# Scratch of the spectra laid out so that one DMA of 128 partitions loads each uin and kin tile; residual loaded in pieces

## The chip, the cores and the metric

One core of one Trainium2 chip runs the program. The metric is device time in microseconds (us) of one execution; lower is better. The core's engines are TensorE (PE, with its weight loads PEld), VectorE (DVE), ScalarE (ACT), GpSimd (POOL, idle here but for the first 2 us) and SyncE (SP), which here does nothing but issue DMAs. Each engine works through its own list of instructions in order; an instruction that waits holds everything behind it on that engine, DMA issues included.

## The reference, cut to what matters

```python
x = A_u                                        # 1 x 2048 x 512, f32
xn = layernorm(x)
# branch A: state-space convolution, done in the reference with an FFT over 2L = 4096
K = einsum("dn,dnl,dn->dl", Cc, exp(dt*A*l), dt*Bc).real     # 512 x 2048, from 128 complex states
s = irfft(rfft(pad(xn.T)) * rfft(pad(K)))[:, :L].T + xn * Dskip
# branch B: a token-mixing block and an MLP
h  = gelu(layernorm(xn) @ w1)                  # 512 -> 512
hs = concat(shift(h, +1), shift(h, -1), shift(h, +2), shift(h, -2), by quarters of D) @ w2
x1 = xn + hs
b  = x1 + gelu(layernorm(x1) @ w3) @ w4        # 512 -> 1376 -> 512
out = x + s * silu(b)
```

## The kernel before, in words

Tokens are split as token = (t, r, s): 32 rows of partitions t for each of r = 0..3, and 16 steps s in the free dimension, so that the tile `X` (128 x 16 x 512) holds the whole activation. The program is recorded by a `Plan` and then issued in the order of a table of numbers (`ORDER`, one number per recorded operation); a letter behind a number says whether a copy or scaling runs on ACT or on DVE. That table decides what stands behind what on every engine. It was made for this program, and the change brings a new one.

The stages overlap by that table. (1) `loads`, layer norm, `h_pair` (w1 and gelu), `u_stage1`: the first step of the Fourier transform of the input by a small matrix `ks1`, copied out as `ue` and stored to the DRAM scratch `Ud`. (2) `hs_pair` (w2), weights w3 and w4 split into two f16 parts (`prep`), then the MLP: eight groups of 256 tokens (`mlp`), each with six steps of w3 (PE tile `pb`, gelu `g`, split `ghl`) and w4 (PE tile `pa`). (3) `tables(0)`, `tables(1)`: for each of the two halves of the channels (256 channels, "half 0" and "half 1"), eight chunks of 32 channels. DVE and ACT build the waves `wv`, PE sums them over the states (`pc`), the result `kev` goes through `ks1` on PE, is copied to `k1e` and stored to the scratch `K1d[half]`, called `scr_Kfa` and `scr_Kfb` in the profile. Two stores per chunk write 4096 runs of 64 bytes each. (4) `products(0)`, `products(1)`: units over the 32 frequencies g. Each unit loads constants `cst` (from `c_gp` for half 0, `c_gq` for half 1, two buffers in turn), `uin` from `Ud` and `kin` from `K1d`. PE forms the two spectra (half 0: `pd` from `kin` and `uin`; half 1: f16 parts `kx` and `uh`, into `pc`), ACT or DVE copies one spectrum to `kh`, DVE multiplies (`pr`), PE runs the first step of the inverse (`pd<-pr,cst`), the result `z1e` is stored to `Zd` (`scr_Zda`, `scr_Zdb`). Half 0 has 16 units of one block, half 1 has 8 units of two blocks. (5) `gate`: silu of the MLP's result in `X`; `inverse`: `zin` is loaded from `Zd`, PE runs the last step (`pd` or `pc` from `zin,is`), DVE multiplies it into `X`; `finish`: DVE adds the residual `xr` (loaded again from the input) and SP and ACT store to the output. MLP work (`pb`, `pa`) fills PE between the steps of stages 3 to 5.

A scratch tensor is one name to the planner: a load from `scr_Kfb` stands behind all sixteen stores to `scr_Kfb`. So half 1 can't load a `kin` before the last chunk of `tables(1)` has landed.

The lines that the prediction's steps touch are 450 to 454 (the scratch), 565 to 566 (buffers of `zin` and `xr`), 804 to 809 (stores of `k1e`), 844 to 852 (loads of `uin` and `kin`), 960 to 975 (`residual` and `finish`), 1121 to 1134 (`u_stage1`) and 1314 to 1323 (the end). Instructions are recorded in one helper, so the profile gives line 330 for nearly all of them and they are told apart by tile.

Of the kernel before, what the change touches and what calls it, by code (L numbers as in the profile page):

```python
# [54 lines left out]
def shape_constants():  # L55
# [10 lines left out]
    c["c_ks1"] = np.tile(np.stack([np.cos(a1), -np.sin(a1)], axis=2).reshape(L1, 2 * NG), (4, 1))  # L66
# [50 lines left out]
8 19 6 39 3 86 7 1086 2 4 44 0 1 21 5 89 90 87 88 91 92 93 94 95 22 20 10 96 97v 23 9 98a 107 108 102v 105 106  # L117
109 110 111 99a 100 101a 103 104a 145 24 26 25 27 18 35 11 33 112 34 32 113 114 115v 117v 123 124 125 116v 118
168 166 164 170 167 119a 120a 28 30 29 31 142 121 126 122a 169 165 16 13 171 143 127 172 14 173 128 174 46 129
175 176 47 177 144 48 130 146 147 178a 180a 181v 179v 78 148 79a 281 285 283 287 149a 131 152a 153a 204a 185v  # L120
150a 284 132 188 282 288 182v 133 286 134 289 201v 155 189 135 290 15 159 224 291 220 225 136 183 222 221 186
191 192 226 223 190 184a 292 187a 154 227 151 52 228 138a 536 229 537 43 230 293 231 49 366 232 50 294 233 51
194 234 53 193 295 235v 54 199a 236a 198a 368 200 207 297v 140v 210 243v 238v 195a 55 56 205 202 59 208 57 58
141 60 237v 206a 364 538 203a 196a 211 264a 367 239v 137 209 369 213 212 296v 61 217a 218a 197 162 17 247 12 374
240 244 219 365 370 62 241a 304a 245a 260a 214a 248 249 215v 63 246 298v 250 251 67 242 139 68 161 216 45 64 69
300v 253 70 539 257v 268 80 269 65 541 261 375 258a 265 252 270 262v 72 259 271 272 299v 263 371 266a 254a 255a
267 37 81a 274 71 273 163 66 73 278v 74 279v 308 84 321v 256 41 301 305 542 76 40 275v 372 160 276v 309 280 277
302v 380 75 306v 311 312 546 303 544 307 547 325v 77 36 314 313 156 319a 310 570 82 83a 315a 316a 318v 320 332
322 323a 317 373 549 85v 326 333 334 329 540 327v 324 378 548 328 345 346 543 157 550 347 571 551 552 554 553
335 42 339v 572 362 336v 358 330 430 376 337v 340v 338 348 350a 377 382 558 349a 351 341 432 388 545 158 361 433  # L130
555 573 381 575 574 331 383 363 386 452 352a 379 434 423 384 556 454 359 557 427 560 422 559 439 342 576 561 579
577 562 389 343 563a 424 578 390 387 344 428 564 565 566a 385 353a 391 591 438 567a 431 443 592 392 581 593 580
425 569 568 400 594 597 444 435 582 596 583 595 401 455 393 584a 440 429 394 354 612 402 436 395 456 441 403 445
437 396 453 464 613 614 397 585 598 355 615 446 586 404 616 587a 457 399 442 466 458 398 600 419 416 459 417a
426 405 478 480 406 588a 460 599 356 407 360 618 357 479 465 486 408 447a 418 409 461 448 462 617 410 602 463
483 420a 528a 590 449 475 589 421 529a 530 601 532a 533a 641 476a 619 450a 534 472 412 413 620 621 469 633 501
414 603 604 500 473a 634 487 531 535 643 505 451 635 502 644 474 491 751a 646 638 605a 645 730 497 731 494 732
622 733a 847 606 636 477 637 508 623 639 734 640 488 498a 737 738 607 744 499 514 608a 739 495a 609a 745 610
740a 741 624 625 746 647 626a 509a 752a 755a 735 736 411 742 627 648 831 747a 611 743 510 748 753 515a 649 756a
642 496 667 415 652 766 767 650 759 760 749 628 651 757 750 517 511 754 668 761 516 768 769a 773 629a 762a 774  # L140
653 669 670 655 518a 758 780 781 787 788 630a 512a 782 654 763 764 657 656 775a 673 671 513 519 658 659 688 660a
770 676 689 672 776 765 794 771 795 772 832 830 789 801a 690 661 796 783a 777 816 662 691 631 632 663a 664a 665
674 778 809 779 784 790a 802a 692 675 785 786 817 678 810 677 797a 791 693 805a 679 680 697 803 798 694 811 681a
792 806a 709 710 682 711 807 695 793 812a 804 813 823 492 715 818 683 837 799 696 698 712 666 800 814 824 684a
808 713 819a 714 699 825a 1296 1289 1297 826 716 820 1087 717 718 685a 1298 686 687 1088 1290 1291 1310a 700 701
815 821 822 827 720 1095 702a 1292a 703 704 1097 705a 846 1299a 1100 1092 1303 1304 1089 706a 708 707 1098 719
1091 1090 829 1293 467 828 1300 481 1311a 1093 721 722 723a 724 468 1312 863 848 1318 1094 1294 1295 1313 1301
725 1099 1319 1109 1101 1305 1122 1102 1314a 1306a 726a 727a 1307 484 729 1096 1315v 728 1302 1320 1332 1325
1326 1123 470 1308 1309 1321v 1316 1322 485 1106 1124 1103 1105 1104 1317 1107 833 834 493 1108 489 1128 1333
1125 1327 1328a 1323 1324 1329 1111 1110 1127 1346 1347 1339 1340 835 865 1330 1331 849 1334a 866 836a 850 838  # L150
864 482 490 1126 1348 839 471 520 840 841 1112 1113 1114a 1129 1144 842 521 522 1335 1130 862 844a 843a 845 523
1341 1145 1342a 1146 1368 851 853 1369 852a 1336 1349a 1353 1354 1115 854 855 856 857 1131 1343 879 880 1116
1147 1355 1132 858 859a 1360a 860a 881 861 882 1117 1118a 867 1119a 1121 1133 1338 868a 1350 1337 897 1361a 869
870 871 1134 1135 1166 1362 1364a 1136a 895 1137 878 872 1344 1345 1363 873 1356v 1351 1167 1120 1150 1153 1168
1149 1138 874 876a 1139 1357 875a 885 898 896 911 1148 883 913 894 884a 877 1169 1171 886 1352 888 1375 887 889
1376 1358 890 1365a 1151 506 1170 1366 1367 1152 1172 1154 1155 891a 892a 1359 1370 901 1140a 899 1377 927 914
929 1382 900a 1141a 902 893 903 1143 904 905 1383 1371a 1196 1389 910 1378a 1396 1390 912 1173 1372 906 907a
908a 1156 1188 1157 1189 909 1158a 915 1174 917 943 916a 1190 1397 1373 1374 930 1159 1160 1175 1379 918 920 926
928 1198 1199 919 1384v 921 1197 1201 1191 945 1142 922 923a 924a 925 946 1161 931 961 944 1385 1176 1177 932a
1200 1162a 933 1391 942 1380 1163a 959 960 934 936 1193 1165 935 937 1194 1192 1195 1381 1386 938 940a 939a 1398  # L160
1202 1178 1179 1392a 947 977 1203 1388 1387 1164 949 962 1204 1403 1393 978 1210 958 941 975 948a 1418 1404 950
952 951 953 1410a 1223 1207 1205 1206 1224 1405 1225 1399v 1400 507 954 955a 1419 1394 1395 1411v 963 976 956a
974 993 1412 1414a 965 1425 1401 1402 1180a 1208 957 964a 966 1181 967 969 1406a 1226 968 1182 1420 991 1407
# [268 lines left out]
def kernel(  # L432
# [41 lines left out]
    class Ring:  # L474
# [3 lines left out]
        def __call__(self, shape, dt, name):  # L478
            o = self.o + self.size * (self.k % self.bufs)
            self.k += 1  # L480
            return at(o, shape, dt, name)
# [869 lines left out]
```

## Time and profile before

| | |
|---|---|
| three runs | 550.22, 554.72, 553.86 us; median 553.86 us |
| the profiled execution | 549.37 us, span of the core 547.6 us, mean granted TensorE clock 0.994 |
| busy: PE, DVE, ACT | 520.5, 491.8, 429.2 us |
| DMA | 91.40 MB in 210781 packets, 155104 of them under 512 bytes |
| HBM | 56.96 MB read, 29.36 MB written |
| issues on SP | `uin` 48 and `kin` 48, `scr_Ud` 16, `scr_Kfa` and `scr_Kfb` 32, `xr` 8 |

The span is what lies between the first and the last instruction of the core in the profile; the time of that execution is 1.8 us longer. Busy times are unions of an engine's instructions. A timeline row reads: start, duration, engine, line, operation, output and inputs, count, and in brackets how long the engine had been idle before it and what released it. Where a row stands for several instructions, its duration runs from the start of the first to the end of the last, and the next row can begin a little before that end, since matmuls are pipelined.

### The profile page before, as it was taken

The numbers are of one execution on the slowest core, as the hardware profiler recorded it, in microseconds if no ns is written. First come the engines' busy times: TensorE is split into PE (matmuls) and PEld (weight loads), VectorE is DVE, ScalarE is ACT, GpSimd is POOL, SyncE is SP. The second block draws the span as 40 slices with busy tenths as digits, with TensorE's granted clock in tenths as the row PEclk, the third lists the DMA queues.
The fourth block names the chain that finished last, engine by engine and source line by source line (L and its number), as shares of the span: only waits on it lengthen the run. The fifth ranks groups of instructions, "written<-read, shape, count | busy, mean of one in ns | idle before, by whom it ended". The sixth has DMA issues, their size and how long they took to land.

```text
span 547.6 us, 13679 instructions
## 1 busy us (share of the span) xinstructions
PE 520.5 (95%) x5660; PEld 336.6 (61%) x5660; DVE 491.8 (90%) x757; ACT 429.2 (78%) x695; POOL 0.7 (0%) x6
## 2 busy tenths in 40 slices
PE   8999989999999999999999999989999999998983
PEld 8787764544476765666656666655566666766540
DVE  4899999999999999999999899989984999896657
ACT  4799999868999999999889889967766366464630
POOL 0000000000000000000000000000000000000000
PEclk9999999999999999999999999999999999999997
DMA  8986763265847236464376676696689988997996
GB/s 213 208 266 217 232 229 125 85 118 134 135 144 145 41 40 59 60 97 60 117 122 146 135 140 173 139 143 107 134 174 170 297 261 240 294 254 224 311 293 192
DMA packets 210781, 91.40 MB, mean 167 GB/s; under 512 B 155104, under 2 KB 196064, under 8 KB 210336
## 3 DMA queue, kind: packets, MB, share of 16 engines
q1 hardware_dynamic: 206112, 86.08, 66.4%
q10 hardware_dynamic: 4608, 4.46, 2.8%
q8 instruction: 44, 0.72, 0.6%
q14 instruction: 17, 0.14, 0.1%
HBM read 56.96 MB, written 29.36 MB: 158 GB/s over the span
## 4 chain that ended last, share of the span: by engine, by line
PE 45%; DVE 21%; DMA 13%; ACT 12%; SPq 4%; issue 3%; DVEq 0%; ACTq 0%
PE pb L330 15%; PE pa L330 14%; PE pc L330 9%; PE pd L330 7%; DVE wv L330 5%; SPq L330 4%; DVE X L330 4%; ACT mag L330 4%; DMA X<-in_A_u_dram 4%; DMA cst<-c_gq 3%; DVE tm L330 2%; ACT L330 2%; DMA out_dram<-X 2%; DVE pr L330 1%; DMA scr_Zda<-z1e 1%
## 5 line engine op out<-in xcount | busy, mean ns | idle before, releaser
L330 PE MATMUL pb<-x1T,w3h 128*128 128x256 f16 (+1 forms) x1056 | 124.0, 273 | 2.0 <-ACT g L330 1.3
L330 PE MATMUL pa<-w4h,ghl 128*128 128x512 f16 (+1 forms) x528 | 121.9, 379 | 0.0
L330 PEld LDWEIGHTS <-w3h 128*128 128x128 f16 (+1 forms) x1056 | 102.1, 100 | 29.1 <-issue 14.8
L330 PEld LDWEIGHTS <-ghl 128*128 128x128 f16 (+1 forms) x528 | 49.7, 98 | 57.8 <-issue 5.3
L330 ACT ACT_TABLE_LOAD x57 | 73.1, 1283 | 2.6 <-PEq L1339 1.7
L330 ACT ACTIVATE wv<-wv 128x2080 f32<-128x2080 int32 x32 | 62.9, 1964 | 5.5 <-DVE wv L330 5.3
L330 ACT ACTIVATE g<-pb,wsc 128x512 f32<-128x512 f32 (+1 forms) x48 | 31.1, 652 | 10.7 <-PE pb L330 9.8
L330 DVE TENSOR_TENSOR wv<-wv,eg 128x2048 f32<-128x2048 f32 x16 | 36.5, 2283 | 0.0
L330 DVE TENSOR_TENSOR wv<-mag,wv 128x2048 f32<-128x2048 f32 x16 | 36.5, 2281 | 0.0
L330 PE MATMUL pd<-pr,cst 64*128 64x256 f32 x256 | 36.3, 402 | 0.0
L330 DVE SCALAR_TENSOR_TENSOR ghl<-g,wsc,ghl 128x512 f16<-128x512 f32 (+1 forms) x48 | 33.6, 699 | 2.8 <-ACT ghl L330 2.7
L330 PE MATMUL pc<-wv 128*32 128x64 f32 x2048 | 32.6, 220 | 2.4 <-issue 2.4
L330 PEld LDWEIGHTS pc<-wv 128*32 128x32 f32 x2048 | 29.8, 109 | 7.7 <-issue 5.8
L330 ACT ACTIVATE ghl<-g,wsc 128x512 f16<-128x512 f32 (+1 forms) x37 | 25.3, 687 | 10.9 <-PE pa L330 9.9
L330 ACT ACTIVATE mag<-par 128x128 f32<-128x128 f32 x132 | 33.1, 454 | 0.0
L330 ACT COPY z1e<-pd 128x256 f32<-128x256 f32 x51 | 17.2, 376 | 20.2 <-PE pd L330 17.4
L330 ACT ACTIVATE wv<-wv,halfpi 128x2080 f32<-128x2080 f32 x16 | 32.9, 2057 | 0.1
L330 ACT ACTIVATE kh<-pc,ksc 128x256 f32<-128x256 f32 (+1 forms) x37 | 18.2, 541 | 18.6 <-PE pc L330 12.6
L330 PE MATMUL pb<-xT,w 128*128 128x256 f32 x128 | 29.9, 384 | 0.7 <-ACT xT L330 0.7
L330 PEld LDWEIGHTS pd<-pr,cst 64*128 64x128 f32 x256 | 22.2, 186 | 10.9 <-issue 7.5
L330 DVE BATCH_NORM_STATS2 stats<-X 128x6 f32<-128x512 f32 x32 | 21.2, 680 | 7.1 <-DMA X<-in_A_u_dram 7.1
L330 PEld LDWEIGHTS pb<-xT,w 128*128 128x128 f32 x128 | 23.4, 190 | 6.5 <-ACT hT L330 1.1
(167 smaller groups left out, 905.5 us busy)
## 6 DMA issues: line engine op xcount, KB each, us to landing
wst<-in_B_w_dram SPq DMA_DIRECT2D x20, 512.0 KB, 4.4
scr_Ud<-ue SPq DMA_DIRECT2D x16, 512.0 KB, 3.2
scr_Kfa<-k1e SPq DMA_DIRECT2D x16, 256.0 KB, 6.3
uin<-scr_Ud SPq DMA_DIRECT2D x32, 128.0 KB, 2.9
cst<-c_gp SPq DMA_DIRECT2D x16, 256.0 KB, 3.1
kin<-scr_Kfa SPq DMA_DIRECT2D x32, 128.0 KB, 2.7
scr_Zda<-z1e SPq DMA_DIRECT2D x16, 256.0 KB, 3.4
scr_Kfb<-k1e SPq DMA_DIRECT2D x16, 256.0 KB, 5.9
```

The costliest lines, as they stand in the source:

```text
L330: ins = [getattr(self.engines[op.eng], name)(*args, **kw).ins for name, args, kw in op.calls]
```

## The change

`Ud` becomes [half, r, s, re/im, g, 256 channels] instead of [r, s, g, re/im, 512 channels]. `K1d` becomes [i, re/im, g, 256] instead of [g and re/im, i, 256]. The constant `ks1` gives its rows in the same order (all real parts, then all imaginary ones). With that, the partition index of `uin` and `kin` is one dimension of the scratch, so one DMA of 128 partitions replaces two of 64, and two (half 0) or four (half 1) frequencies lie side by side: rows of 2 and 4 KB where they were 1 KB. For it, each `ue` is stored by two DMAs with 1 KB rows instead of one with 2 KB rows, and the 64-byte runs of a `k1e` store now lie 64 KB apart along i instead of 1 KB. The residual of a half comes in four pieces of four steps instead of two of eight; half 0 has two buffers for them and three (not four) for `zin`. All operations have a new order.

```diff
-    c["c_ks1"] = np.tile(np.stack([np.cos(a1), -np.sin(a1)], axis=2).reshape(L1, 2 * NG), (4, 1))
+    c["c_ks1"] = np.tile(np.stack([np.cos(a1), -np.sin(a1)], axis=1).reshape(L1, 2 * NG), (4, 1))
...
 ORDER = """
-8 19 6 39 3 86 7 1086 2 4 44 0 1 21 5 89 90 87 88 91 92 93 94 95 22 20 10 96 97v 23 9 98a 107 108 102v 105 106
+2 5 4 0 6 8 7 86 22 21 20 23 9 10 27 87 89 88 24 26 90 25 3 91 19 11 92 93 39 18 28 31 29 30 34 35 32 33 94 16
...
-    Ud = dram.tile([4, S, NG, 2, D], F32, name="scr_Ud")
-
     DH = D // 2
-    K1d = [dram.tile([2 * NG, L2, DH], F32, name=f"scr_Kf{h}") for h in "ab"]
+    Ud = dram.tile([2, 4, S, 2, NG, DH], F32, name="scr_Ud")
+
+    K1d = [dram.tile([L2, 2, NG, DH], F32, name=f"scr_Kf{h}") for h in "ab"]
...
-    zinr = [Ring(early, K4, 4), Ring(o, K4, 8)]
-    xrs = [early + 4 * K4, o + 13 * K4, late, late + 2 * K4]
+    zinr = [Ring(early, K4, 3), Ring(o, K4, 8)]
+    xrs = [Ring(early + 3 * K4, K4, 2), Slots(o + 13 * K4, o + 14 * K4, late, late + K4)]
...
             Q.dma_start(
-                K1d[cc // 8][:, :, ch : ch + 16],
+                K1d[cc // 8][:, :, :, ch : ch + 16].rearrange("i e g d -> (e g) i d"),
                 k1e[64 * c : 64 * c + 64].rearrange("p i n d -> p i (n d)"),
             )
...
-            for e in range(2):
-                Q.dma_start(
-                    uin[e::2],
-                    Ud[:, :, g0 : g0 + 2 * nb, e, ch].rearrange("r s g d -> (r s) g d"),
-                )
+            Q.dma_start(uin, Ud[hf][:, :, :, g0 : g0 + 2 * nb].rearrange("r s e g d -> (r s e) g d"))
             kin = ring["kin"]([P, 2 * nb, DH], F32, "kin")
-            halves_of = K1d[hf][2 * g0 : 2 * g0 + 4 * nb].rearrange("(k e) i d -> e i k d", e=2)
-            for e in range(2):
-                Q.dma_start(kin[e::2], halves_of[e])
+            Q.dma_start(kin, K1d[hf][:, :, g0 : g0 + 2 * nb].rearrange("i e g d -> (i e) g d"))
...
-    def residual(hf):
+    def residual(hf, pieces):
         ch = slice(hf * DH, hf * DH + DH)
-        for k in range(2):
+        for k in pieces:
             due(f"xr{hf}.{k}")
-            xr = at(xrs.pop(0), [P, S // 2, DH], F32, "xr")
-            by_r(xr, xv[:, :, k * S // 2 : (k + 1) * S // 2, ch], load=(Q, A))
-            resid.append(xr)
+            xr = xrs[hf]([P, 4, DH], F32, "xr")
+            by_r(xr, xv[:, :, 4 * k : 4 * k + 4, ch], load=(Q, A))
+            resid[hf, k] = xr
...
-            Q.dma_start(
-                Ud[2 * rp : 2 * rp + 2, s : s + 2].rearrange("r s g e d -> (s g e) r d"), ev_t
-            )
+            for h in range(2):
+                Q.dma_start(
+                    Ud[h, 2 * rp : 2 * rp + 2, s : s + 2].rearrange("r s e g d -> (s e g) r d"),
+                    ev_t[:, :, h * DH : (h + 1) * DH],
+                )
...
     for hf in range(2):
-        residual(hf)
+        residual(hf, (1, 2) if hf == 0 else (1, 2, 3, 0))
         for k, g in enumerate(END_ORDER):
...
+            if hf == 0 and k in (1, 3):
+                residual(hf, (3,) if k == 1 else (0,))
```

`Slots` hands out the given places one after the other, as `Ring` does for a ring of buffers.

Three places of the new order. First, SP's list where half 0 ends and half 1 begins: `scr_Kfb<-k1e` are the stores of the last chunks of `tables(1)`, `uin` and `kin` with 64 or 128 partitions are the loads of the first units of half 1. Before:

```order
L330 DMA scr_Kfb<-k1e 4096x1x16
L330 DMA scr_Zda<-z1e 128x512
L330 DMA scr_Kfb<-k1e 4096x1x16
L330 DMA cst<-c_gq 128x1024
L330 DMA_TRANSPOSE x1T<-x1h 128x8x128
L330 DMA scr_Zda<-z1e 128x512
L330 DMA uin<-scr_Ud 64x4x256 x2
L330 DMA scr_Kfb<-k1e 4096x1x16 x2
L330 DMA uin<-scr_Ud 64x4x256 x2
L330 DMA kin<-scr_Kfb 64x4x256
L330 DMA uin<-scr_Ud 64x4x256
L330 DMA kin<-scr_Kfb 64x4x256
```

And now:

```order
L330 DMA cst<-c_gq 128x1024
L330 DMA uin<-scr_Ud 128x1024 x2
L330 DMA_TRANSPOSE x1T<-x1h 128x8x128
L330 DMA scr_Zda<-z1e 128x512
L330 DMA scr_Kfb<-k1e 64x64x16 x2
L330 DMA uin<-scr_Ud 128x1024
L330 DMA kin<-scr_Kfb 128x1024 x2
L330 DMA xr<-in_A_u_dram 32x4x256
L330 DMA kin<-scr_Kfb 128x1024
```

Two whole `uin` now stand ahead of the last two stores of `k1e` where one did, and one issue instead of two brings a whole `kin` behind them.

Second, SP's list in the middle of half 1, where `cst` has two buffers in turn. Before:

```order
L330 DMA scr_Zdb<-z1e 128x1024
L330 DMA uin<-scr_Ud 64x4x256
L330 DMA cst<-c_gq 128x1024
L330 DMA uin<-scr_Ud 64x4x256
L330 DMA kin<-scr_Kfb 64x4x256
L330 DMA uin<-scr_Ud 64x4x256
L330 DMA_TRANSPOSE x1T<-x1h 128x8x128
L330 DMA uin<-scr_Ud 64x4x256 x2
L330 DMA kin<-scr_Kfb 64x4x256
L330 DMA cst<-c_gq 128x1024
```

And now:

```order
L330 DMA uin<-scr_Ud 128x1024 x2
L330 DMA kin<-scr_Kfb 128x1024
L330 DMA cst<-c_gq 128x1024
L330 DMA uin<-scr_Ud 128x1024
L330 DMA scr_Zdb<-z1e 128x1024
L330 DMA xr<-in_A_u_dram 32x4x256
L330 DMA kin<-scr_Kfb 128x1024
L330 DMA cst<-c_gq 128x1024
```

Between two loads of constants stood six halves of `uin` and `kin`; now there are one `uin` and one `kin`, and a piece of the residual among them.

Third, the end of DVE's list, from the last sums of the MLP on (`X<-pa,wsc,X`; `X<-X,pd` and `X<-X,pc` multiply one step of the inverse into `X`, `X<-X,xr` adds the residual). Before, the first 12 of 28 rows:

```order
L330 SCALAR_TENSOR_TENSOR X<-pa_93,wsc,X 128x512
L330 SCALAR_TENSOR_TENSOR X<-pa_92,wsc,X 128x512
L330 TENSOR_TENSOR X<-X,pd_99 128x256
L330 TENSOR_TENSOR X<-X,pd_98 128x256
L330 TENSOR_TENSOR X<-X,pc_97 128x256
L330 TENSOR_TENSOR X<-X,pc_96 128x256
L330 TENSOR_TENSOR X<-X,pd_98 128x256
L330 TENSOR_TENSOR X<-X,pd_99 128x256
L330 TENSOR_TENSOR X<-X,pc_96 128x256
L330 TENSOR_TENSOR X<-X,pc_97 128x256
L330 TENSOR_TENSOR X<-X,pd_98 128x256
L330 TENSOR_TENSOR X<-X,xr 128x4x256
```

And now, the first 12 of 20:

```order
L330 SCALAR_TENSOR_TENSOR X<-pa_92,wsc,X 128x512
L330 SCALAR_TENSOR_TENSOR X<-pa_93,wsc,X 128x512
L330 TENSOR_TENSOR X<-X,pd_98 128x256
L330 TENSOR_TENSOR X<-X,pd_99 128x256
L330 TENSOR_TENSOR X<-X,xr 128x2x256
L330 TENSOR_TENSOR X<-X,pc_97 128x256
L330 TENSOR_TENSOR X<-X,pc_96 128x256
L330 TENSOR_TENSOR X<-X,xr 128x4x256
L330 TENSOR_TENSOR X<-X,pc_97 128x256
L330 TENSOR_TENSOR X<-X,pc_96 128x256
L330 TENSOR_TENSOR X<-X,xr 128x4x256
L330 TENSOR_TENSOR X<-X,pc_96 128x256
```

Behind the last sums of the MLP stand twelve multiplications and six sums where there were twenty and six; the eight others, and the four steps of the inverse that feed them, have moved ahead.

More of the change, by code (lines that the diff above doesn't have):

```diff
@@ L122 @@
[L122 to L136, printed above, removed]
@@ L481, in __call__, with __init__ @@
             return at(o, shape, dt, name)
+    class Slots:
+        def __init__(self, *places):
+            self.places = list(places)
+        def __call__(self, shape, dt, name):
+            return at(self.places.pop(0), shape, dt, name)
     ident = keep([P, P], "ident")
```

147 lines of the change are left out of this document (80 added, 67 removed), and 7 rows, old and new, of the table ORDER.

## The prediction

> **What bounds the kernel now.** I read the head of the page first: which engine has the least room.
>
> ```profile
> span 547.6 us, 13679 instructions
> PE 520.5 (95%) x5660; PEld 336.6 (61%) x5660; DVE 491.8 (90%) x757; ACT 429.2 (78%) x695; POOL 0.7 (0%) x6
> ```
>
> PE is busy for 520.5 of 547.6 us, so all that can be won is 27.1 us. A busy PE could still be a slow PE, so next I read its timeline over one unit of half 1.
>
> ```profile
> 484.52 0.84 PE L330 MATMUL pc<-kx,cst 128*64 128x256 f16 x12 [0.27 <-DMA cst<-c_gq]
> 485.20 0.82 PE L330 MATMUL pc<-uh,cst 128*64 128x256 f16 x12
> 485.95 1.13 PE L330 MATMUL pd<-pr,cst 64*128 64x256 f32 x8
> 487.02 1.49 PE L330 MATMUL pb<-x1T,w3h 128*128 128x256 f16 x12
> 488.44 0.85 PE L330 MATMUL pc<-kx,cst 128*64 128x256 f16 x12
> ...
> 489.87 1.47 PE L330 MATMUL pa<-w4h,ghl 128*128 128x512 f16 x6
> 491.27 1.13 PE L330 MATMUL pd<-pr,cst 64*128 64x256 f32 x8
> 494.48 0.85 PE L330 MATMUL pc<-kx,cst 128*64 128x256 f16 x12 [2.08 <-DMA cst<-c_gq]
> ```
>
> Groups start as soon as the one ahead ends: 0.68 us for twelve spectrum matmuls, 0.75 with the change of shape, 1.07 for an inverse step, 1.42 for twelve `pb`, 1.40 for six wide `pa`. The change leaves PE's instructions as they are, form by form; it only moves them. So the time is 520.5 us plus PE's idle time. Where that lies comes from the windows of the end.
>
> ```profile
> 520.00:535.00 15.00, 12.94 (x144) 6.21 (x142) 8.73 (x17) 4.63 (x6) 0.00 (x0) 1.00 0.84 273
> 535.00:548.00 13.00, 3.48 (x64) 0.96 (x64) 8.71 (x17) 0.00 (x0) 0.00 (x0) 0.71 0.70 202
> ```
>
> PE is idle for 2.1 + 9.5 = 11.6 us there, and for 15.5 us in the 520 us before. The biggest gaps of those 15.5, besides 0.27 and 2.08 above, are in these timeline rows:
>
> ```profile
> 71.01 0.66 PE L330 MATMUL pc<-ident,pn 128*128 128x128 f32 x4 [1.19 <-DVE wv L330]
> 82.37 3.70 PE L330 MATMUL pb<-w,hT 128*128 128x512 f32 x8 [0.70 <-ACT hT L330]
> 307.37 1.08 PE L330 MATMUL pd<-kin,cst 128*64 128x256 f32 x8 [1.00 <-DMA cst<-c_gp]
> 367.91 0.53 PE L330 MATMUL pc<-wv 128*32 128x64 f32 x20 [2.36 <-issue]
> 432.03 0.74 PE L330 MATMUL pc<-kx,cst 128*64 128x256 f16 x10 [0.97 <-DVE kx L330]
> 476.39 0.85 PE L330 MATMUL pc<-kx,cst 128*64 128x256 f16 x12 [0.44 <-DMA cst<-c_gq]
> ```
>
> Waits that DMAs end make 3.8 us (1.00, 0.44, 0.27, 2.08). **The change can win at most a few us on transfers**, since nearly all of them are hidden behind a full PE.
>
> **The loads, part by part.** What a load costs stands in the list of DMA issues (count, size, median from issue to landing).
>
> ```profile
> kin<-scr_Kfa SPq DMA_DIRECT2D x32, 128.0 KB, 2.7
> cst<-c_gp SPq DMA_DIRECT2D x16, 256.0 KB, 3.1
> kin<-scr_Kfb SPq DMA_DIRECT2D x16, 256.0 KB, 4.8
> cst<-c_gq SPq DMA_DIRECT2D x8, 512.0 KB, 5.5
> scr_Kfb<-k1e SPq DMA_DIRECT2D x16, 256.0 KB, 5.9
> ...
> 421.56 0.58 SPq L330 DMA_DIRECT2D kin<-scr_Kfb  x1
> ```
>
> The new `uin` and `kin` have the shape of `cst`: 128 rows of 2 or 4 KB. So I price them with `cst`: 3.1 us for half 0, 5.5 us for half 1. Two halves, the second issued 0.6 us (0.58) behind the first, land after 2.7 + 0.6 = 3.3 and 4.8 + 0.6 = 5.4 us. The pair and the single load land alike; 48 issues of some 0.6 us go away on SP, 16 (`ue` stored in two) and 8 (`xr`) come.
>
> The Trainium skill ("DMA: Bandwidth & Descriptors", Rules for kernel authors) says that two transfers to disjoint halves of the partitions serialize and should be one. If it were so here, a pair would take 2 x 4.8 = 9.6 us by the row, and where a `kin` is waited for the single load would win 4.1 us; the rows of `cst` and the 0.58 us issue let me take 0 of it.
>
> *Waits for constants, -2.0 us.* A `cst` load can start when its buffer's last inverse step is done, so it has to land while PE works on one other unit. The chain of waits and the timeline show the longest case:
>
> ```profile
> 487.15 7.28 DMA cst<-c_gq
> ```
>
> From 487.15 PE had work until 491.27 + 1.13 = 492.4, 5.25 us, and the load took 7.28. Counting the new PE order with the durations above gives, at the six hand-overs of half 1, 5.0, 5.0, 6.3, 6.3, 5.0 and 4.6 us of PE work (before: 5.0 to 5.3 at all six). Two get 1.3 us more room, and fewer issues stand ahead of each `cst` on SP. Bounds: all 3.8 us go, or the 4.6 us place and a piece of `xr` cost 1.0 more. I take half of the gain, -2.0.
>
> *The stall "issue" at 367.91, -1.0 us.* It lies inside one run of matmuls, while SP was held up by two stores of 64-byte runs:
>
> ```profile
> 363.19 4.82 SPq L330 DMA_DIRECT2D scr_Kfb<-k1e  x2
> ```
>
> Those stores keep their 4096 runs each, but all else is reordered. Bounds 0 (it comes again) and -2.4; I take -1.0, nearer to 0, since the stores stay.
>
> *Lighter ACT and DVE, -1.0 us.* Table loads fall from 57 to 52, and three `uh` scalings leave DVE:
>
> ```profile
> L330 ACT ACT_TABLE_LOAD x57 | 73.1, 1283 | 2.6 <-PEq L1339 1.7
> L330 DVE TENSOR_SCALAR uh<-uin 128x1024 f16<-128x1024 f32 x6 | 4.0, 686 | 3.9 <-DMA uin<-scr_Ud 3.9
> ```
>
> That is 5 x 1.28 = 6.4 us on ACT and 3 x 0.69 = 2.1 us on DVE, hidden as long as PE is full. Only PE's waits for these two can shrink: 1.19 + 0.70 = 1.9 us at 71 and 82 us. Bounds 0 and -1.9; I take the middle, -1.0.
>
> *From half 0 to half 1, +1.5 us.* Here the stores of the last chunk must land before `kin` is loaded, and PE needs other work meanwhile. The rows of PE, SP and DVE:
>
> ```profile
> 408.46 1.09 PE L330 MATMUL pc<-kev,ks 32*64 32x512 f32 x8
> 430.78 0.28 PE L330 MATMUL pc<-kx,cst 128*64 128x256 f16 x2
> ...
> 412.88 3.82 SPq L330 DMA_DIRECT2D scr_Kfb<-k1e  x2
> ...
> 430.69 1.28 DVE L330 SCALAR_TENSOR_TENSOR kx<-kin,ksc,kx 128x1024 f16<-128x1024 f32 x1
> ```
>
> Last sums of the chunk until 409.5, stores issued from 412.88, first `kin` issued 421.56 (8.7 us later), both parts of `kx` ready at 432.0. PE had 430.78 - 409.5 = 21.3 us of other work and waited 0.97. In the new order 24 `pb` and six `pa` fewer stand between the two places; by the prices above that is 2 x 1.42 + 1.40 = 4.2 us less: 17.1 us. The new chain: 3.4 (to the first store) + 8.7 (to the issue of `kin`) + 5.5 (one `kin`, by `c_gq`) + 2.0 (`kx`, 1.28 for its second part and 0.75 for its first) = 19.6 us, so PE waits 2.5 us where it waited 0.97. That `uin` is now loaded ahead of the stores removes DVE's 3.9 us wait (the `uh` row above), which PE's work hid. Bounds: -1.0 (no wait left) and +5.0 (both transfers at 7.28 us or more); I take +1.5. What stands behind the `kin` on SP meanwhile: two pieces of `xr`, a `cst` and an `x1T`, which are needed later.
>
> *Last units of half 1, +1.5 us.* There the new order leaves less PE work between a spectrum and its inverse step, in which ACT copies and DVE multiplies. The block whose second spectrum stood at 495.16 had its inverse step 3.9 us after it:
>
> ```profile
> 495.16 0.82 PE L330 MATMUL pc<-uh,cst 128*64 128x256 f16 x12
> 499.82 1.13 PE L330 MATMUL pd<-pr,cst 64*128 64x256 f32 x8
> ```
>
> Nowhere was it under 3.7 by the same count. The last three blocks now have 3.1, 2.4 and 1.6 us. If each needs 3.7, PE waits 0.6 + 1.3 + 2.1 = 4.0 us; if the earlier copy of `kh` is enough, 0. I take +1.5.
>
> *The end, -1.2 us.* The last `pa`, the DVE work behind it and the price of its parts:
>
> ```profile
> 522.39 6.64 PE L330 MATMUL pa<-w4h,ghl 128*128 128x512 f16 x30
> 528.96 0.66 PE L330 MATMUL pd<-zin,is 64*32 64x256 f32 x16
> ...
> 529.07 1.41 DVE L330 SCALAR_TENSOR_TENSOR X<-pa,wsc,X 128x512 f32<-128x512 f32 x2 [4.26 <-PE pa L330]
> ...
> 543.06 0.69 DVE L330 TENSOR_TENSOR X<-X,xr 128x512 f32<-128x512 f32 x1
> ...
> L330 DVE TENSOR_TENSOR X<-X,pd 128x256 f32<-128x256 f32 x16 | 6.3, 412 | 2.7 <-PE pd L330 2.7
> L330 DVE TENSOR_TENSOR X<-X,xr 128x1024 f32<-128x1024 f32 x7 | 8.5, 1218 | 0.0
> ```
>
> DVE works from 529.07 to 543.75, and 3.85 us later the span ends (the last stores). Eight multiplications fewer stand there now: 8 x 0.41 = 3.3 us. The four inverse steps that feed them now run on PE ahead of the last `pa`; sixteen matmuls of one step take 0.66 us alone (528.96) and overlap with their neighbours, so I put 0.5 us on each, 2.1 us in all, an estimate. Net -1.2. Bounds: -3.3 (the four fall into gaps) and +2 (stores of 0.5 MB now follow each other every 1.9 us and pile up).
>
> *Other pieces, +0.3 us.* Sixteen more stores of `ue` (0 to +2; the early PE is full). Fewer buffers for `zin`: 0, since `inverse` of half 0 starts late. The residual in pieces: 0, hidden by the MLP.
>
> Sum: -2.0 - 1.0 - 1.0 + 1.5 + 1.5 - 1.2 + 0.3 = -1.9 us. Against the profiled execution, 549.37 us, that is 547.5, or -0.35%. The median of the three runs is 553.86 us, 0.8% above the profiled one, so the forecast on that scale is 551.9 us.
>
> **The rivals.** (a) *The transfers bring all they can*: -3.8 - 2.4 - 1.9 - 1.0 - 3.3 = -12.4 at the bounds; two thirds of it, -8, gives 546. For it: fewer issues, `uin` early. Against: each of these gaps lies elsewhere and a new order opens others.
>
> (b) *The 64-byte runs get slower*, the other side. In a store of `k1e` they now lie 64 KB apart, not 1 KB. No row shows such a pitch for short runs; `cst` and `kin` rows show wide ones only. If landing goes from 5.9 to 11.8 us, both places where a first `kin` waits for last stores (the start of half 0 and of half 1) pay 5.9: +11.8 - 1.9 = +9.9, or 563.8 us. It decides (over 1%) from 2 x d - 1.9 = 5.5, d = 3.7, a landing of 9.6 us.
>
> The Trainium skill ("DMA: Bandwidth & Descriptors", Latency and other measured facts) tells of row pitches at large powers of two: 207 GB/s at 512 KiB, 103 at 4 MiB, 214 with padding. By that rule 64 KB costs nothing and the sum stays; no run here shows a pitch that large.
>
> (c) *The thinner cover*: both upper bounds at the start and the end of half 1 (+5.0, +4.0) and no gain for `cst`: -1.9 + 3.5 + 2.5 + 2.0 = +6.1, or 560 us. For it: 17.1 us against a chain of 19.6. Against: `kin` in one issue.
>
> **How the numbers follow.** A measurement of this kernel tells about 1% from no change. My forecast, within 1%: 0.42. (a): 0.33. (b): 0.10, (c): 0.15, together slower 0.25. The range leaves out the last tenth on each side: 542 (all of (a)'s bounds) to 563 (nearly (b)); the likeliest case's own is 548.3 to 559.4.
>
> **What the profile after would show.** PE busy near 520 us. `kin` landing near 5.5 us and `scr_Kfb` near 6. PE waits for `cst<-c_gq` under 1.5 us in all. A wait before the first `kx` of half 1 of 2 to 3 us. 15 us from the last `pa` to the end instead of 18.6. Wrong if `scr_Kf` stores land after 9.6 us or more, or if PE's idle time ahead of the last `pa` leaves 10 to 22 us.

## The result and the profile after

The change is faster: 541.19 us (539.90 to 542.27) against 552.04 us of the kernel before on the same chip, a ratio of 0.9867, 95% interval 0.9837 to 0.9897. Timed again with the experiments, it was 0.9896 (0.9876 to 0.9916). The profiled execution took 541.05 us where that of before took 549.37, so 8.3 us are to be explained. The forecast was 547.5 us on that scale. In the experiments, on four chips, the kernel before took 546.4 to 547.9 us at the median, less than in its profile, so 1.5 to 3 of the 8.3 us may belong to the one execution of it that was profiled.

The head of the page after:

```profile
span 539.3 us, 13674 instructions
PE 520.4 (97%) x5660; PEld 335.9 (62%) x5660; DVE 489.1 (91%) x750; ACT 425.9 (79%) x697; POOL 0.7 (0%) x6
```

PE is as busy as before (520.5 us), so all of the 8.3 us are waits of PE: 27.1 us of them before, 18.9 now. These rows of PE's timeline after bear on the steps of the prediction (in brackets the wait and what ended it):

```profile
70.83 6.71 PE L330 MATMUL pb<-xT,w1h 128*128 128x256 f16 x60 [1.10 <-ACT hT L330]
80.61 3.70 PE L330 MATMUL pb<-w,hT 128*128 128x512 f32 x8 [0.61 <-ACT hT L330]
203.63 0.31 PE L330 MATMUL pc<-wv 128*32 128x64 f32 x5 [0.92 <-issue]
399.59 0.30 PE L330 MATMUL pc<-wv 128*32 128x64 f32 x3 [1.23 <-issue]
475.42 0.85 PE L330 MATMUL pc<-kx,cst 128*64 128x256 f16 x12 [0.40 <-DMA cst<-c_gq]
483.88 0.84 PE L330 MATMUL pc<-kx,cst 128*64 128x256 f16 x12 [0.23 <-DMA cst<-c_gq]
526.00 0.67 PE L330 MATMUL pc<-zin,is 64*32 64x256 f32 x16 [1.88 <-DVE X L330]
```

The waits for constants have all but gone (3.8 us before, 0.63 now), the first `kx` of half 1 is not waited for, and the stall named "issue" came again at two other places. The windows say the same by stretch; the columns are the window, its length, the busy time of PE, PEld, DVE, ACT and POOL, the granted clock, the DMA share and GB/s:

```profile
300.00:400.00 100.00, 98.54 (x1409) 63.84 (x1406) 97.28 (x124) 86.09 (x150) 0.00 (x0) 1.00 0.73 142
400.00:500.00 100.00, 99.21 (x948) 66.63 (x947) 80.36 (x124) 62.16 (x109) 0.00 (x0) 1.00 0.89 249
520.00:550.00 30.00, 8.44 (x124) 2.51 (x121) 14.30 (x25) 1.06 (x1) 0.00 (x0) 0.76 0.51 149
```

PE was idle for 4.4 us between 300 and 400 us and for 4.2 between 400 and 500 us before; now 1.5 and 0.8. The landings of the loads, in the list of DMA issues:

```profile
scr_Kfb<-k1e SPq DMA_DIRECT2D x16, 256.0 KB, 6.2
cst<-c_gq SPq DMA_DIRECT2D x8, 512.0 KB, 5.0
uin<-scr_Ud SPq DMA_DIRECT2D x8, 512.0 KB, 5.3
kin<-scr_Kfb SPq DMA_DIRECT2D x8, 512.0 KB, 5.8
```

A whole load of half 1 lands about when a pair did (in half 0 a little later: a `kin` in 3.8 us where a half took 2.7 and the second was issued 0.6 us behind it), and the 64-byte runs of `k1e` land as before (6.2 against 5.9 us), so rival (b) is out. What the whole loads do change is SP's time. The lists of one tile's instructions give the time of an issue (ns: shortest, median, longest), of before and then of after:

```profile
L330 SPq DMA_DIRECT2D kin<-scr_Kfb x16: 580/592/977, 421.6 to 471.7; - x16
```

```profile
L330 SPq DMA_DIRECT2D kin<-scr_Kfb x8: 319/424/715, 415.8 to 462.5; - x8
```

One issue of a whole `kin` takes 0.42 us, less than one for every second partition (0.60). For `uin` and `kin` together that is 96 x 0.60 = 58 us of SP before and 48 x 0.42 = 20 us now.

### The profile page after: what moved, and what is told of

Read it like the earlier page. It is cut to its first block, busy times and chain, and to the rows that moved or that the text cites. A ratio compares the mean times of both kernels' runs of the same rounds, so it can differ in the third digit from the quotient of the medians.

```text
span 539.3 us, 13674 instructions
## 1 busy us (share of the span) xinstructions
PE 520.4 (97%) x5660; PEld 335.9 (62%) x5660; DVE 489.1 (91%) x750; ACT 425.9 (79%) x697; POOL 0.7 (0%) x6
## 4 chain that ended last, share of the span: by engine, by line
PE 65%; ACT 14%; DMA 10%; DVE 7%; issue 2%; SPq 1%; ACTq 0%; DVEq 0%
PE pb L330 23%; PE pa L330 20%; PE pc L330 12%; PE pd L330 11%; DMA X<-in_A_u_dram 4%; DVE X L330 3%; ACT mag L330 3%; ACT L330 3%; ACT wv L330 2%; DMA zin<-scr_Zdb 2%; DVE tm L330 1%; SPq L330 1%; DMA zin<-scr_Zda 1%; DMA x1T<-x1h 1%; ACT EB L330 1%
## 5 line engine op out<-in xcount | busy, mean ns | idle before, releaser
L330 PE MATMUL pa<-w4h,ghl 128*128 128x512 f16 (+1 forms) x528 | 123.6, 380 | 0.0
L330 ACT COPY z1e<-pd 128x256 f32<-128x256 f32 x53 | 18.4, 372 | 17.6 <-PE pd L330 16.3
L330 PE MATMUL pb<-w,hT 128*128 128x512 f32 x58 | 26.9, 601 | 0.6 <-ACT hT L330 0.6
```

Of the source, the lines that this page charges most:

```text
L330: ins = [getattr(self.engines[op.eng], name)(*args, **kw).ins for name, args, kw in op.calls]
```

## The experiments

Two theories went in. "Order": the gain comes from the new order of all instructions. "Transfers": it comes from the whole loads. In kernels whose plan skips an empty operation the recording helper is at line 332, not 330.

**The old scratch on the new order, and the new scratch on the old order.** In the first the layouts, the stores and the pairs of loads are those of before, each pair issued where the whole load stands:

```diff
+            with plan.together():
+                for e in range(2):
+                    Q.dma_start(kin[e::2], halves_of[e])
```

> The new order with the old scratch: rows of 1 KB, every uin and kin in two loads of 64 partitions, one store per ue, 64-byte runs 1 KB apart. Theory 'order': the 8.3 us (of the span, 547.6 to 539.3) come from what now stands behind what on PE, ACT, DVE and SP, and a pair of loads lands like one whole load, so this stays within 2 us of the change: a ratio to before of 0.984 to 0.990. Theory 'transfers': the gain needs the whole loads and the 48 issues less on SP, so this falls back to before or behind it: 0.998 or more, with cst waits of 2 us or more in PE's list again. If both are needed, about half of the gain is left: 0.991 to 0.996.

The second is the kernel before with the new layouts, the whole load where the first half stood:

```diff
-            for e in range(2):
-                Q.dma_start(kin[e::2], halves_of[e])
+            Q.dma_start(kin, K1d[hf][:, :, g0 : g0 + 2 * nb].rearrange("i e g d -> (i e) g d"))
+            with plan.together():
+                pass
```

> The old order (and the old residual) with the new scratch: each whole load stands where the first of its two halves stood, each ue is stored by two DMAs. Theory 'order': nothing is won, 0.997 to 1.003; the waits of PE at the old places (2.36 'issue', 2.08 for cst, 0.97 for kx) come again within 1 us. Theory 'transfers': 0.984 to 0.990, and the waits for cst (3.8 us before) shrink to under 1.5 us. By the prediction's own terms (half of the cst waits, no gain elsewhere) 0.996.

Both, and the change, were measured; the last two twice:

| ratio to before, span | old order | new order |
|---|---|---|
| old scratch | 1, 547.6 us | 0.9997 (0.9966 to 1.0028), 547.0 us |
| new scratch | 0.9891 (0.9847 to 0.9934), 541.0 us | 0.9867 (0.9837 to 0.9897), 539.3 us |
| again | 0.9939 (0.9915 to 0.9964), 539.4 us | 0.9896 (0.9876 to 0.9916), 539.5 us |

The new order alone brings nothing, and "order" as the cause of the whole gain falls. The scratch alone brings 0.6 to 1.1%. On the old order PE's large waits (2.36, 2.08, 0.97 us) are gone though nothing but the scratch had changed; of its first timeline, the largest one left between 200 and 520 us, the place of the old stall, and the largest wait for `cst` (its waits for `cst` are 1.6 us in all):

```profile
253.32 5.42 PE L332 MATMUL pb<-x1T,w3h 128*128 128x256 f16 x48 [1.18 <-DMA x1T<-x1h]
365.31 0.54 PE L332 MATMUL pc<-wv 128*32 128x64 f32 x20 [0.17 <-issue]
472.30 0.85 PE L332 MATMUL pc<-kx,cst 128*64 128x256 f16 x12 [0.74 <-DMA cst<-c_gq]
```

Where the kernel before waited 2.08 us, SP had not been late: the inverse step that frees the buffer ended at 487.08 us (485.95 + 1.13), and `cst` was issued at 487.15. It was the landing that took long, 7.3 us. With the scratch alone the matching `cst` was issued at 482.73, as soon after its inverse step (481.52 + 1.14), and landed in 4.9 us. The DMA engines had more to do before it in the kernel before: its last `uin` was issued at 472.30, where with the scratch alone the last load of that kind, a `kin`, went out at 462.02. The windows of 2 us around the issue of the `cst` one earlier show it (columns as above; before, with `cst` issued at 478.99, then the scratch alone, at 474.91):

```profile
478.00:480.00 2.00, 2.00 (x14) 1.01 (x13) 1.64 (x3) 1.33 (x4) 0.00 (x0) 1.00 0.92 323
```

```profile
474.00:476.00 2.00, 2.00 (x14) 0.93 (x12) 1.73 (x3) 1.33 (x4) 0.00 (x0) 1.00 0.20 42
```

The second run of the scratch alone has the same lull (a DMA share of 0.20 from 472 to 474 us, `cst` issued at 473.28). So a busy SP may cost without issuing the urgent load late: the loads before it go out later, and the DMA engines are still full when it comes. No run takes this apart from the rest.

The old scratch on the new order has a long wait for `cst` again, and a second price with it. Its timeline and its windows (PE alone):

```profile
445.85 1.49 PE L332 MATMUL pc<-kx,cst 128*64 128x256 f16 x12 [3.23 <-DMA cst<-c_gq]
```

```profile
446.00:448.00 2.00, 2.00 (x22) 0.50 1.04 392
```

After a wait of 3.23 us the granted clock is 0.50, and twelve matmuls that take 0.85 us take 1.49.

**The whole load in two again.** Is it the rows or the number of loads? Here all is as in the change, but each load comes in two halves:

```diff
-            Q.dma_start(kin, K1d[hf][:, :, g0 : g0 + 2 * nb].rearrange("i e g d -> (i e) g d"))
+            with plan.together():
+                for e in range(2):
+                    Q.dma_start(kin[e::2], K1d[hf][:, e, g0 : g0 + 2 * nb])
```

> The change as it is, rows of 2 and 4 KB, but each uin and kin loaded by two DMAs of 64 partitions, issued one behind the other: 48 more issues on SP of 0.3 to 0.6 us. Theory 'order': hidden, the ratio to before is that of the change within 0.2% (0.985 to 0.989). Theory 'transfers': the single load is part of the gain; with the second half 0.6 us later and later cst issues it gives back 2 to 4 us: 0.991 to 0.995. If two halves ran strictly one behind the other (2 x 4.8 us), kin of half 1 would land after some 9.6 us instead of 5.8, PE would wait 3 to 4 us at the first kx of half 1 and the ratio would be 0.993 or more.

0.9959 (0.9932 to 0.9986), span 543.5 us: 4.2 us of the gain are given back, just above the 2 to 4 us of "transfers". PE's waits for `cst` are 4.0 us in all. The largest of them, on SP, on PE and in the DMA issues from 430 to 444 us:

```profile
423.73 1.30 SPq L332 DMA_DIRECT2D kin<-scr_Kfb  x2
430.39 0.35 SPq L332 DMA_DIRECT2D is<-c_is  x1
...
432.16 2.51 SPq L332 DMA_DIRECT2D uin<-scr_Ud  x4
434.78 1.17 SPq L332 DMA_DIRECT2D kin<-scr_Kfb  x2
436.05 0.54 SPq L332 DMA_DIRECT2D cst<-c_gq  x1
```

```profile
434.00 1.14 PE L332 MATMUL pd<-pr,cst 64*128 64x256 f32 x8
443.09 0.84 PE L332 MATMUL pc<-kx,cst 128*64 128x256 f16 x12 [2.75 <-DMA cst<-c_gq]
```

```profile
cst<-c_gq SPq DMA_DIRECT2D x1, 512.0 KB, 7.0
```

And the same place in the change:

```profile
426.91 1.08 SPq L330 DMA_DIRECT2D uin<-scr_Ud  x2
428.78 0.32 SPq L330 DMA_DIRECT2D kin<-scr_Kfb  x1
434.68 0.33 SPq L330 DMA_DIRECT2D cst<-c_gq  x1
```

```profile
433.51 1.13 PE L330 MATMUL pd<-pr,cst 64*128 64x256 f32 x8
439.78 0.85 PE L330 MATMUL pc<-kx,cst 128*64 128x256 f16 x12
```

```profile
cst<-c_gq SPq DMA_DIRECT2D x1, 512.0 KB, 3.7
```

In the change `uin` and `kin` had been issued 6 us ahead, SP stood free when the inverse step released the buffer (434.64), and `cst` landed in 3.7 us, well within PE's 5.1 us of other work. With halves SP was behind: `cst` left 0.9 us after its buffer was free, right behind six half loads that had left 6 us ahead in the change, and landed in 7.0 us beside them. Two things had put SP behind. The six halves took 2.3 us more of SP than the three whole loads (3.68 against 1.40 us). And SP had stood still from 425.0 to 430.4 us, ahead of the load of `is`, which the change issues at 422.89; the table of waits puts this stop down to an `xr`:

```profile
SPq L332 <- DMA xr<-in_A_u_dram: 9.8, 5, 5.4
```

What an `xr` has to do with `is` shows in the run without bytes below.

**Four quarters.**

```diff
+                for r in range(4):
+                    Q.dma_start(
+                        kin[32 * r : 32 * r + 32],
+                        K1d[hf][16 * r : 16 * r + 16, :, g0 : g0 + 2 * nb].rearrange("i e g d -> (i e) g d"),
+                    )
```

> The change as it is, but each uin and kin loaded by four DMAs of 32 partitions: 144 more issues on SP, of 0.35 to 0.45 us some 50 to 65 us of SP's time. It asks how much room the new order has for issues. Theory 'order': most of it is hidden, since SP waits for buffers most of the time; 0.2 to 0.8% above the change (0.988 to 0.995). Theory 'transfers': issues ahead of cst, kin and x1T are what PE waits for; three times the cost of the halves, 6 us or more: 0.998 or more.

1.0262 (1.0219 to 1.0305), span 558.9 us, as "transfers" had it: there is little room for issues. The loss is 19.6 us where the halves lose 4.2, so it grows faster than their number. Not all of it is waiting: PE is busy for 527.4 us instead of 520.4, since after several waits its granted clock stood at 0.50.

**Halves of neighbouring partitions** (`kin[64 * h : 64 * h + 64]` in place of `kin[e::2]`).

> The change as it is, each uin and kin loaded by two DMAs of 64 neighbouring partitions, not of every second one. An issue of every second partition took 0.59 us at the median, one of 32 neighbours or of all 128 took 0.42: if it is the stride that is dear, these halves take 0.42, and SP gives 20 us more than in the change (48 x 0.42) where the strided halves gave 37 (96 x 0.59 less 48 x 0.42). Theory 'SP's time': the loss lies between the change (0.987) and the strided halves (0.996): 0.989 to 0.994. Theory 'number of loads' (each load's own start and end count, not its issue): as the strided halves, 0.994 to 0.998. Theory 'stride' (the whole loss is the strided side): as the change, 0.985 to 0.989.

1.0140 (1.0102 to 1.0178), outside all three. The issue was hardly cheaper (median 0.49 to 0.59 us), so the stride alone is not what makes it dear. The landings of all loads of half 1 got longer (`uin` 6.1 us; in the strided halves `uin` 4.9, `kin` 5.4, `cst` 5.0 us):

```profile
cst<-c_gq SPq DMA_DIRECT2D x8, 512.0 KB, 6.3
kin<-scr_Kfb SPq DMA_DIRECT2D x16, 256.0 KB, 6.3
```

With as many loads as the strided halves and no more time of SP, this costs 10.1 us of span instead of 4.2. So neither the number of loads nor SP's issue time alone sets the loss. Why neighbours land later was not found.

**The constants issued by GpSimd**, in the kernel before and in the change: if SP's queue makes `cst` late, a queue of its own should help.

```diff
-            Q.dma_start(cst.rearrange("p n a b c -> p n (a b c)"), ...
+            G.dma_start(cst.rearrange("p n a b c -> p n (a b c)"), ...
```

> The kernel before with one thing changed: the 24 loads of cst are issued by GpSimd, which is idle, not by SP. Theory 'SP's time': PE waits for cst because uin and kin stand ahead of it on SP; those waits (3.8 us in the profile of before) fall under 1 us, and SP has 24 issues less: 0.990 to 0.995. Theory 'busy DMA engines': cst is late because the DMA engines are full there (0.9 to 1.07 of their time), whoever issues it: the waits stay near 3 to 4 us and the ratio at 0.998 to 1.002. If GpSimd's issue itself takes 2 us longer than SP's, the waits grow: above 1.002.

> The changed kernel with the loads of cst issued by GpSimd. Only 0.63 us of waits for cst are left there, so by the theory 'SP's time' little can be won: the change's ratio or 0.1% under it, 0.985 to 0.988. If an issue from GpSimd is slower than one from SP, or disturbs DVE, it is behind the change: 0.989 or more, with waits for cst of more than 1 us.

1.0200 (1.0148 to 1.0253) and 1.0020 (0.9989 to 1.0052): worse in both, the case that the texts had kept for a dearer issue by GpSimd. PE's waits for `cst` grew from 3.8 to 8.2 us and from 0.63 to 4.0 us. The longest wait in the first, on GpSimd and on PE, with the DMA issues from 470 to 480 us:

```profile
471.53 1.39 POOL L330 DMA_DIRECT2D cst<-c_gq  x1 [9.89 <-PE pd L330]
```

```profile
480.17 1.10 PE L330 MATMUL pc<-kx,cst 128*64 128x256 f16 x12 [3.86 <-DMA cst<-c_gq]
```

```profile
cst<-c_gq POOLq DMA_DIRECT2D x1, 512.0 KB, 8.6
uin<-scr_Ud SPq DMA_DIRECT2D x1, 256.0 KB, 10.1
```

GpSimd begins this issue 0.45 us after the inverse step that frees the buffer (469.95 + 1.13 us), where SP began 0.07 us after, and takes 1.39 us for it (0.53 at the median). Meanwhile SP, now free of `cst`, sends less urgent loads into the same DMA engines. A likely reading is that one queue in the right order is also a priority; no run tests it alone, and how much of the loss is GpSimd's own issue can't be told from these two.

The Trainium skill ("DMA: Bandwidth & Descriptors", Issuing engines are not separate DMA queues) says that starting DMAs on several engines saves only the time of the issue, which is usually small beside the DMA. One issue is small here too (0.33 us of SP for a `cst` that lands in 5.0 us), and moving them away won nothing. What many issues on one queue cost together is another question, and the next run asks it.

**Issues without bytes.** The cleanest test: the change, and behind every `uin` and `kin` two loads of 8 bytes into a tile that is no longer read.

```diff
+    def small():
+        for _ in range(2):
+            junk.append(junk.pop(0))
+            Q.dma_start(junk[-1], u[0, 0:1, 0:2])
```

> The change as it is; behind every uin and kin two more DMAs of 8 bytes each, into a tile that nothing reads: 96 more issues on SP and next to no bytes. At 0.3 to 0.45 us each they take 29 to 43 us of SP, about the 37 us that the strided halves take more than the change. Theory 'SP's time' (what stands behind the loads on SP comes later): as the strided halves, 0.993 to 0.999, with waits of PE for cst of 2 to 4 us again. Theory 'transfers' (rows, spread over the partitions, DMA engines): as the change, 0.985 to 0.989.

0.9988 (0.9960 to 1.0016), span 543.5 us, that of the strided halves, with the wait for `cst` back. The issue time of the small loads (tile `rs`), PE's wait, and the chain of waits ahead of it:

```profile
L332 SPq DMA_DIRECT2D rs<-in_A_u_dram x96: 223/249/349, 155.8 to 467.5; - x96
```

```profile
442.90 0.85 PE L332 MATMUL pc<-kx,cst 128*64 128x256 f16 x12 [3.50 <-DMA cst<-c_gq]
```

```profile
428.94 5.22 DMA xr<-in_A_u_dram
...
434.18 0.24 SPq L332
...
436.59 6.26 DMA cst<-c_gq
```

So DMAs cost even without bytes. Their number is not the measure either: 96 of these cost what 48 more loads cost in the strided halves (a span of 543.5 us in both). The chain shows one way in which they cost: SP held a small load back until an `xr` had landed with which it shares no tile. SP's list in the program names the semaphores that each issue waits for (of the change, from 434.68 us on):

```
L330 DMA cst_560<-c_gq 128x1024 [waits DMAHW1_49,PE_49]
L330 DMA uin_591<-scr_Ud_60 128x1024 [waits DMAHW2_49,DVE_49]
L330 DMA scr_Zdb_64<-z1e_545 128x1024 [waits DMAHW3_49,Activation_49]
L330 DMA xr_620<-in_A_u_dram 32x4x256 [waits DMAHW4_49]
L330 DMA kin_592<-scr_Kfb_62 128x1024 [waits DMAHW5_49,DVE_49]
L330 DMA cst_570<-c_gq 128x1024 [waits DMAHW7_49,PE_49]
```

The numbers of the DMA semaphores run from 0 to 7 in turn (6 is missing here; ACT issues loads of `xr` in between). As list and chain read together, an issue that takes a semaphore again waits until the DMA that had it eight issues earlier has landed, be it of SP or of ACT: the `xr` of the chain was issued by ACT. A load cut in two thus takes two of eight places, and a load of ACT can hold up SP. The table of waits shows what SP waited for `xr`: 3.4 us in the change (2.0 at the longest), 9.8 in the strided halves (5.4), 7.8 here (4.3). The load of `is` in the halves waits in the program for nothing but such a place. So where `cst` was latest there, this stop was the larger part of SP's delay: 5.4 us, against 2.3 us that the added issues took. For the whole loss, how much is issue time (96 x 0.25 = 24 us of SP) and how much these places was not taken apart. In the kernel before, SP waited only 1.0 us for `xr`, so at least this stop is not what the whole loads win there.

**The short runs.** The stores of `k1e` go to 64 rows of 4 KB; the kernel leaves out the transposition.

```diff
-                K1d[cc // 8][:, :, :, ch : ch + 16].rearrange("i e g d -> (e g) i d"),
-                k1e[64 * c : 64 * c + 64].rearrange("p i n d -> p i (n d)"),
+                K1d[cc // 8][8 * (cc % 8) + 4 * c : 8 * (cc % 8) + 4 * c + 4].rearrange(
+                    "i e g d -> (i e g d)").rearrange("(p x) -> p x", p=64),
+                k1e[64 * c : 64 * c + 64].rearrange("p i n d -> p (i n d)"),
```

> The change with the stores of k1e written as 64 rows of 4 KB in place of 4096 runs of 64 bytes: left out is the transposition on the way to the scratch, so half the spectrum's values stand in other places. It asks what the short runs still cost. If they are hidden behind PE's work, the ratio stays at 0.986 to 0.988. If they hold up SP (3.3 to 4.1 us for a pair of stores) so that something waits, and if PE's two stalls named 'issue' (0.92 and 1.23 us) come from them, the stalls go and the first kin of half 1 comes some 5 us earlier: 0.979 to 0.984.

0.9893 (0.9862 to 0.9924), span 539.6 us. The stores land in 3.4 us in place of 6.2, and the time stays. The "issue" stalls stay too, this one and one of 0.74 us at 203.84:

```profile
399.73 0.30 PE L330 MATMUL pc<-wv 128*32 128x64 f32 x3 [1.34 <-issue]
```

**Residual sums on GpSimd**, tried as a better version: `finish` gives four sums of the end to GpSimd.

```diff
+    POOLED = {(1, 1), (1, 3), (1, 5), (0, 7)}
...
-                finish(hf, *ENDS[hf][k])
+                finish(hf, *ENDS[hf][k], pool=(hf, k) in POOLED)
```

> The changed kernel with four of the last residual sums (1.22 us each on DVE) given to GpSimd, which is idle. From the last MLP sum (522.5 us) to its last store DVE has no gap, and PE's last inverse steps wait for it. If DVE's list bounds the end, up to 4 x 1.22 = 4.9 us come free; GpSimd's own sums then run beside DVE: 1.5 to 4 us won, 0.980 to 0.985. If a GpSimd sum takes over 4 us, or slows DVE down by as much, nothing is won or some is lost: 0.986 to 0.995. If the stores bound the end: as the change, 0.987.

0.9915 (0.9887 to 0.9943), span 539.7 us: not better than the change. GpSimd takes 2.4 us for a sum that DVE does in 1.22, and ends at 534.5 us, where DVE had ended:

```profile
524.76 9.71 POOL L330 TENSOR_TENSOR X<-X,xr 128x1024 f32<-128x1024 f32 x4 [523.45 <-DVE X L330]
```

**Does the new order add to the scratch?** The change and the scratch alone once more, on one chip.

> The changed kernel once more, beside the new scratch on the old order, on one chip. If the scratch brings all of the gain, both stand at the same ratio to before within 0.3%. If the new order adds to it (spans of 539.3 and 541.0 us so far), this one is 0.3% or more ahead: about 0.987 against 0.990.

> The new scratch on the old order once more. If the new order adds to the gain: 0.990, 0.3% or more behind the change. If the new order adds nothing: the change's ratio within 0.3%. Waits of PE at the old places as in the first run of it (cst 1.6 us, x1T 1.2 us, none at the first kx of half 1) would show that its trace is no chance.

0.9896 and 0.9939: the change is ahead by 0.4%, and by 0.2% in the first pair. Here the two ran on one chip and can be compared directly: 540.7 to 541.3 us in four runs against 540.7 to 545.5 in nine, means 541.0 and 543.1. The difference, 2.0 us, is four times its standard error (0.5 us, worked out from these thirteen times), so with the new scratch the new order does add something, though alone it brought nothing. That the two spans in the table are equal (539.5 and 539.4 us) is chance: the scratch alone was profiled in the second fastest of its nine runs. In the second run of the scratch alone the waits for `cst` were 0.35 us, for `x1T` 1.26 us, and none at the first `kx`.

## Where the prediction held and where it failed

The direction was right and the size was not: the sum gave 1.9 of 8.3 us, and the likeliest case, "within 1%", did not come. Rival (a) did, for which the text gave 546 us. On the prediction's scale the result is 0.9867 x 553.86 = 546.5 us, inside the range; the measured 541.19 us itself lies just under its low end, 542. The second measurement would give 0.9896 x 553.86 = 548.1 us, at the edge of the likeliest case (548.3). That (a)'s number was met so well is in part luck: its own five terms won 5.4 us, not 8, and the rest came from places that it does not name. Terms in us, with the change of PE's wait in the two profiles:

| step | predicted | measured |
|---|---|---|
| waits for constants | -2.0 | -3.2 (3.8 to 0.63) |
| stall "issue" | -1.0 | -0.7 (2.36 + 0.45 to 0.92 + 1.23) |
| lighter ACT and DVE, at 71 and 82 us | -1.0 | -0.2 (1.89 to 1.71) |
| half 0 to half 1 | +1.5 | -1.0 (0.97 to 0) |
| last units of half 1 | +1.5 | 0 |
| the end | -1.2 | -0.3 (PE's wait from 520 us on: 11.2 to 10.9) |
| the rest | +0.3 | -2.9 |
| sum | -1.9 | -8.3 |

*The step that failed is the first one on the loads*: "The pair and the single load land alike". In half 1 they do (`kin` 5.8 us where 5.5 was foreseen; in half 0 it took 3.8 where 3.1 was foreseen), but the merged load's own landing was the wrong measure. The text saw the 48 issues go and gave them a value only for `cst`, and half of the waits there. The run of 8-byte loads shows what DMAs cost without their bytes: 24 us of issues, with the places that they take, cost 4.2 us of span and bring back a wait for `cst` of 3.50 us. And where the kernel before waited longest for a `cst`, its landing was slow though its issue was not late (7.3 us, 4.9 with the scratch alone). How much each way of costing adds to the 8.3 us stays open.

In the last row of the table, PE's waits for ACT (`z1e`, `g`) behind the first 100 us, 2.8 us before and 0.6 after, had no term at all. They have two causes. Those for `z1e` fell with the scratch alone, from 1.6 to 0.5 us; why a `z1e` comes earlier when SP has less to do was not followed further. Those for `g` did not (1.25 us before, 1.35 and 1.58 with the scratch alone) and went only with the new order, to 0.3. Another 0.7 us of that row lie before 40 us, where one kernel differs by as much from run to run (PE idle for 2.4 us in the change, 1.8 when it was profiled again).

*Half 0 to half 1.* One link of the chain was mis-sized. From the last sums to the first store it took 3.4 us before, and the text carried that over. The second copy of `k1e` ran on DVE there, behind other work:

```profile
412.14 0.68 DVE L330 COPY k1e<-pc 128x512 f32<-128x512 f32 x1
```

After (PE, ACT and SP):

```profile
404.90 1.09 PE L330 MATMUL pc<-kev,ks 32*64 32x512 f32 x8
423.30 0.82 PE L330 MATMUL pc<-kx,cst 128*64 128x256 f16 x12
...
406.08 1.07 ACT L330 COPY k1e<-pc 128x512 f32<-128x512 f32 x2 [0.44 <-ACT z1e L330]
...
407.18 3.56 SPq L330 DMA_DIRECT2D scr_Kfb<-k1e  x2
415.76 0.81 SPq L330 DMA_DIRECT2D kin<-scr_Kfb  x2
```

It is 1.2 us now (406.0 to 407.18): the 3.4 us were queues on ACT and DVE, not the cost of the copies, and the new order lets ACT make both copies of `k1e` at once. From store to `kin` it took 8.6 us (8.7 foreseen), from `kin` to `kx` on PE 7.5 (7.5 foreseen). The sum, 17.3 us, is what PE had of other work (17.1 foreseen), and the wait is zero.

*Last units.* The thin covers were enough: the whole of 400 to 500 us holds 0.79 us of idle PE, 0.63 of them for `cst`. The second bound, that the earlier copy of `kh` is enough, was right.

*The end.* From the last `pa` (ends at 523.1 us) to the end it took 16.2 us, where 15 was foreseen and 18.6 stood before. The steps behind it wait for DVE's sums, as the row at 526 us shows; with those sums taken away, GpSimd and the stores end no earlier. The prediction's split of the idle time is off by 0.4 us, since its last window reaches to 548 us, past the end of the span: 11.2 us of PE's idle time lie after 520 us and 15.9 before, not 11.6 and 15.5. Nothing else hangs on it.

*The stall "issue"* shrank but came again elsewhere, as the bound 0 had it. The text put it down to the 64-byte stores; with wide stores it is still there, so that reading is refuted, and its cause is open.

## What to carry to other kernels

Price a merge of DMAs by what its queue no longer has to do, not by when the merged load lands: look up what stands ahead of each load that PE waits for, what one issue takes in each form, what else is in the DMA engines when that load comes, and how many DMAs the program can have in flight. Loads of a few bytes behind the real ones show what issues cost by themselves. A delay read from the old order may be a queue on another engine, so look what stands ahead of the step in the new order before carrying it over.

## What the runs showed of the hardware

- An issue of a whole `uin` or `kin` (128 partitions) took 0.42 us at the median in the change, one of a half (64 partitions, strided or neighbouring) 0.49 to 0.61 us, one of 8 bytes 0.25 us. The reason for the dear half was not found.
- In half 1, halves on 64 neighbouring partitions landed in 6.1 to 6.3 us, on every second partition in 4.9 to 5.4, whole loads of twice the size in 5.3 to 5.8. The Trainium skill ("DMA: Bandwidth & Descriptors", Rules for kernel authors) says that two transfers to disjoint halves serialize. By these medians no pair took twice its half: 6.3 us and an issue of 0.6 us at the most, against 5.8 whole.
- 64-byte runs 64 KB apart landed like those 1 KB apart (5.9 and 6.2 us against 6.3 and 5.9).
- PE's granted clock went to 0.50 after waits of 3.23 us (the old scratch on the new order), 2.67 and 3.98 us (the quarters) and 3.50 us (the 8-byte loads, 1 to 2 us after the matmuls had begun again), and stayed at 1.00 after 2.75 us (the strided halves). The window of the 8-byte loads (after 2.67 us in the quarters it is 0.50 from 362 to 364 us):

```profile
445.00:446.00 1.00, 1.00 (x6) 0.72 (x5) 0.49 (x1) 1.00 (x3) 0.00 (x0) 0.50 0.80 240
```

  So the length of the wait alone does not decide. The Trainium skill ("TensorE: Matmul & The Clock Gate", What's actually happening) gives an idle window of about 3.4 us that runs freely, not from the start of the wait. That the shorter of two waits can be the one that halves the clock agrees with a window that runs freely; that 2.67 and 3.23 us were enough does not agree with 3.4 us of full idleness.
